# A fused sparse-attention and gated-FFN kernel: first gate weights in two column pieces, 52 constant matmuls in a new order, the last product in halves

## The chip, the cores and the metric

The kernel runs on one core of a Trainium2 chip. The metric is the device time of one execution in microseconds. Before the change three runs gave a median of 281.0 us (280.67 to 282.69). One more execution was recorded by the hardware profiler; it took 279.88 us, with a span of 278.2 us from the first to the last instruction.

TensorE (PE) multiplies matrices, VectorE (DVE) and ScalarE (ACT) do elementwise work and move results out of the accumulator banks, GpSimd (POOL) does elementwise work more slowly, and SyncE (SP) issues most transfers. Transfers run in queues: SP's loads and stores in one (q1 in the profile), the weight loads that POOL issues in another (q0).

## The reference

Two steps follow each other. The first is causal attention over 4 batches, 8 heads, 768 positions and a head size of 64, in which every query sees only six chunks of 32 keys:

- per chunk the minimum and the maximum of each key component are taken; a bound for query and chunk is `sum(max(q * k_min, q * k_max))`
- per query the six chunks with the highest bounds among those not ahead of it are kept
- softmax of `q k^T / 8` over the kept chunks and the causal positions, times `v`

The heads are put side by side, so that there are 3072 rows `x` of 512. The second step is a gated feed-forward layer, `(sigmoid(x @ w_gate) * (x @ w_val)) @ w_out`, with 1536 features.

## The kernel before

**Units.** The 3072 rows are cut into eight units of 384. Unit 0 holds the first 128 rows of batches 0, 1 and 2; for these every chunk is among the kept six, so they need no selection (`first`, line 699). The other units take three blocks of 128 rows each. A unit goes through: turning keys and queries so that the head dimension lies on the partitions (transposes `kT`, `qT`, for unit 0 `kfT`, `qfT`), bounds and choice of chunks (`ub`, `ubn`, `mx`, `ap`, `apt`), scores (`sc`), exponentials on ACT (`exp`), the causal mask on POOL (`cm`), the product with the values (`pv`), division (`rz`, `x`), a turn of the result (`xps` and `xT`; for units 3 to 7 a DMA transpose issued by SP), and the feed-forward layer (`ffn`, line 1239).

**Feed-forward layer.** The 1536 features are 12 blocks of 128. For each there is a gate product `g` and a value product `v` of four matmuls (384 columns), a tanh on ACT in place of the sigmoid, and a product on DVE (`hg`, line 1280). Then `o` multiplies by `w_out`. Units 5 to 7 compute the gate blocks 2 to 9 in pairs with seven block products instead of eight (`by7`). Units 4 to 7 compute the output by a seven-product scheme as well (`pair`, line 1058): once for two row blocks of the unit, and for the third blocks of two units together (`u45`, `u67`). A scheme's products are p1, p2 and p6, p5, p3, p7, p4; each is evacuated by an addition on DVE onto an array of four quarters (`c11`, `u4`, `c12`, `c22`, `c21`), and the last of all is p4 of `u67`, then `c21`, then the last store.

**Loads.** SP loads raw k, q and v. POOL issues the weight loads, which turn float32 into float16 on the way: `wgp` and `wg0` (the first four gate blocks), `wv0`, `wv1`, `wg1`, `wv2`, `wg2`, then `wo0` to `wo2`. `wg`, `wv` and `wo` with a number are 512 columns (or 4 blocks of 128 rows) each.

**Constant matmuls.** `keep_awake` (line 589) adds 30 matmuls of a constant with itself, named `fl`. Their results aren't read; they only keep PE at work while the first data come.

**What sets the order.** Each operation is named and added to a plan with its reads and writes. Three written tables then decide: `ORDER` (line 96) gives the order in which all operations are issued and the engine of each, `SLOTS` the buffer slot of each buffer, and `TIES` adds waits of one operation for another. Every engine works through its own part of `ORDER` in that order; dependencies are kept by semaphores. So a name's place in `ORDER` is its place in its engine's queue, and a waiting operation holds all behind it on its engine.

In the order before, PE starts with nine constant matmuls; then the transposes of the first keys and queries, the first scores and the other constant matmuls follow. The first gate products are `g_u0_0` and `g_u0_2`, then the bounds of unit 1 (`ub_u1`), `g_u0_3`, `g_u0_1`, and the value products from `v_u0_1` on. On POOL `wgp` stands between two causal masks of the first unit, and `wg0` and `wv0` three operations later, behind `hkf0`.

Of the kernel before, what the change touches and what calls it, by code (L numbers as in the profile page):

```python
# [96 lines left out]
ident=G ones16=V fl_4=P fl_2=P fl_8=P fl_3=P fl_1=P fl_0=P fl_29=P k2_u1=S kn_u1_2=A qf1_0=S kf1_0=S kf0_0=S fl_6=P fl_5=P epat0=V  # L97
ident16=V ap0=V epat=G hkp110=A hkp000=A hkp001=V kT_u1_2=P kcr0=V kt_u1_2=V hk0_u1_2=G vf1_1=G hkp011=V hkp010=G vf1_2=G hkp100=G
kf1_2=S kf0_1=S kfT_0=P kxf1=V fl_17=P fl_10=P fl_7=P kx0_u1_2=V kf16_0=V qf0_0=S qfT_0=P qf16_0=V qf1_1=S kf1_1=S kfT_1=P
kf16_1=V fl_15=P fl_16=P scf_0=P expf_0_1=A fl_19=P qf0_1=S qfT_1=P hq0=V ap1=V fl_14=P fl_9=P fl_13=P fl_11=P fl_18=P fl_12=P  # L100
qf16_1=V scf_1=P v10=G vf_0=S v16_0_0=G qf0_2=S qf1_2=S kf0_2=S expf_0_0=A cmf_0_0=G pvf_0_0=P rzf_0_0=V xf_0_0=V kx1_u1_2=V
cmf_0_1=G wgp=G kfT_2=P pvf_0_1=P qfT_2=P qf16_2=V rzf_0_1=V xf_0_1=V kxf0=V expf_1_0=A cmf_1_0=G vf_1=S vc_1=G pvf_1_0=P
rzf_1_0=V xpsf_0_0=P expf_1_1=A cmf_1_1=G pvf_1_1=P hkf0=G hk1_u1_2=A kf16_2=A scf_2=P expf_2_1=A expf_2_0=A k0_u1=S kn_u1_0=V
kT_u1_0=P xf_1_0=V fl_20=P fl_21=P wg0=G q3_u1=S qn_u1_3=A q2_u1=S rzf_1_1=V xf_1_1=V xpsf_1_1=P hq1=V xTf_1_1=V kx0_u1_0=V
kx1_u1_0=V vf_2=S wv0=G cmf_2_0=G fl_23=P xpsf_0_1=P fl_24=P fl_22=P fl_27=P xpsf_1_0=P vc_2=G xTf_1_0=V pvf_2_0=P rzf_2_0=V
xf_2_0=V q1_u1=S k3_u1=S kn_u1_3=G kT_u1_3=P hkp111=A q0_u1=S fl_28=P kx1_u1_3=V cmf_2_1=G pvf_2_1=P xpsf_2_0=P rzf_2_1=V xf_2_1=V
qT_u1_3=P qf_u1_3=V k1_u1=S qn_u1_1=A qT_u1_1=P xTf_0_0=A xTf_0_1=A qn_u1_2=A qn_u1_0=A kn_u1_1=G kT_u1_1=P kx1_u1_1=V kx0_u1_1=V
kt_u1_0=A qm_u1_3=A fl_25=P xpsf_2_1=P fl_26=P qT_u1_2=P v_0_3=S v_0_2=S v_0_1=S qf1_3=S k0_u2=S q2_u2=S k1_u2=S qf_u1_1=V
qf_u1_2=V v11=G wv1=G wg1=G hq0_u1_3=G qT_u1_0=P kt_u1_3=A hk0_u1_3=G hq1_u1_3=G wv2=G xTf_2_1=A xTf_2_0=A qf_u1_0=A qm_u1_0=A
g_u0_0=P g_u0_2=P kx0_u1_3=V kcr_f=V kcr_u1=V hkp101=V hq1_u1_0=V hkf1=V kt_u1_1=V hk0_u1_1=G wg2=G qm_u1_2=A qm_u1_1=A ub_u1=P  # L110
ubn0_u1=V ubm0_u1=V hq0_u1_1=A hq0_u1_2=A g_u0_3=P g_u0_1=P mx0_u1=V ap0_u1=V apt0_u1=V hqm0_u1_0=V v_u0_1=P v_u0_0=P v_u0_2=P
hq0_u1_0=A tanh_u0_2=A tanh_u0_1=A hg_u0_1=V ubn1_u1=V v_u0_3=P tanh_u0_3=A hg_u0_3=V ubm1_u1=V hg_u0_2=V tanh_u0_0=A hg_u0_0=V
hk0_u1_0=A hq1_u1_1=A sc_u1_0_2=P exp_u1_0_2=A sc_u1_1_2=P sc_u1_0_1=P sc_u1_0_0=P exp_u1_1_2=A sc_u1_1_0=P sc_u1_1_1=P
exp_u1_0_0=A exp_u1_0_1=A v_u0_7=P wo0=G hqm0_u1_2=G sc_u1_2_2=P exp_u1_2_2=A sc_u1_2_0=P exp_u1_2_0=A sc_u1_3_0=P sc_u1_3_2=P
exp_u1_3_2=A exp_u1_1_0=A sc_u1_3_1=P exp_u1_3_1=A exp_u1_3_0=A v16_0_3=G wo1=G v_u0_4=P sc_u1_2_1=P v_u0_6=P exp_u1_2_1=A
hk1_u1_0=G v16_0_2=G wo2=G mx1_u1=V ap1_u1=V apt1_u1=V hqm1_u1_0=V g_u0_5=P tanh_u0_5=A v_u0_5=P exp_u1_1_1=A hqm1_u1_2=A g_u0_6=P
tanh_u0_6=A g_u0_7=P tanh_u0_7=A hg_u0_7=V v16_0_1=G cm_u1_3=G pv_u1_3=P cm_u1_2=G hk1_u1_1=G g_u0_4=P tanh_u0_4=A hg_u0_4=V
vf1_3=G hq1_u1_2=G pv_u1_2=P sc_u1_5_1=P sc_u1_4_2=P sc_u1_4_1=P rz_u1_1=V x_u1_1=V exp_u1_4_1=A v_u0_9=P v_u0_10=P xps_u1_1=P
xT_u1_1=A exp_u1_4_2=A hg_u0_6=V hk1_u1_3=V hg_u0_5=V v_u0_8=P g_u0_10=P tanh_u0_10=A kcr1=V hg_u0_10=V g_u0_8=P tanh_u0_8=A
hg_u0_8=V sc_u1_5_2=P exp_u1_5_2=A g_u0_9=P tanh_u0_9=A hg_u0_9=V sc_u1_4_0=P exp_u1_4_0=A cm_u1_1=G pv_u1_1=P cm_u1_0=G qn_u2_2=G  # L120
sc_u1_5_0=P pv_u1_0=P exp_u1_5_0=A sc_u1_6_1=P exp_u1_6_1=A sc_u1_6_2=P exp_u1_6_2=A exp_u1_5_1=A sc_u1_7_2=P sc_u1_7_0=P
g_u0_11=P qT_u2_2=P sc_u1_7_1=P tanh_u0_11=A exp_u1_7_2=A exp_u1_7_0=A exp_u1_7_1=A kn_u2_1=V kT_u2_1=P rz_u1_0=V x_u1_0=V
xps_u1_0=P cm_u1_5=G pv_u1_5=P cm_u1_4=G pv_u1_4=P qf_u2_2=V q1_u2=S qn_u2_1=V qT_u2_1=P sc_u1_6_0=P kt_u2_1=A exp_u1_6_0=A
kn_u2_0=G kT_u2_0=P kt_u2_0=A v_u0_11=P rz_u1_2=V xT_u1_0=V x_u1_2=V xps_u1_2=P q3_u2=S qn_u2_3=G qT_u2_3=P cm_u1_7=G pv_u1_7=P
# [1332 lines left out]
```

## Time and profile before

| | us |
|---|---|
| median of three runs | 281.0 |
| profiled execution | 279.88 |
| its span | 278.2 |
| PE busy | 269.2 |
| DVE busy | 231.2 |
| ACT busy | 180.4 |
| POOL busy | 163.1 |

A row of the profile names the line in the kernel, the engine, the operation, what it writes and reads (output<-input, buffer numbers left out), and how often it occurs. In a timeline the first number is the start in us, the second the length; square brackets give idle time of the engine ahead of it and what ended it. A waiting row reads "who <- for whom: us in total, times, longest". In the chain that ended last each piece has a start, a length and an engine or transfer. A row of transfers reads: output<-input, issuing engine, count, KB, and the time from issue to landing.

### The profile page before, as it was taken

To read this page: it belongs to the slowest core of one execution; us is meant where nothing else is said; L and a number is where in the kernel's file an instruction comes from. 1 tells how busy PE (TensorE), PEld (TensorE's weight loads), DVE (VectorE), ACT (ScalarE), POOL (GpSimd) and SP (SyncE) were. 2 spreads that over 40 slices of the span, in tenths; PEclk is the share of its full clock that TensorE was granted. 3 is DMA by queue.
4 is the path that set the end of the run, shared out by engine and by line. 5 is a ranking of instruction groups with operands and counts; after the bars stand their busy time and mean duration, and the time that the engine had idled before them with its cause. 6 is when DMAs were issued, how large, how long until landed. Compare 5 with 4: busy or idle time off the path is not lost.

```text
span 278.2 us, 7566 instructions
## 1 busy us (share of the span) xinstructions
PE 269.2 (97%) x2806; PEld 189.3 (68%) x2806; DVE 231.2 (83%) x686; ACT 180.4 (65%) x386; POOL 163.1 (59%) x262
## 2 busy tenths in 40 slices
PE   5979999999999999999999999999999999999995
PEld 3755658667755666557687657776888688778684
DVE  4799747687999998796999987978889998888985
ACT  6388969569858944468689979988983422341430
POOL 5797744639372873534669966724766467163440
PEclk9999999999999999999999999999999999999999
DMA  6999999999999598696896230100320033000304
GB/s 157 258 281 204 207 217 208 220 179 202 187 217 189 142 183 188 145 161 125 164 157 114 68 85 17 40 0 3 73 77 2 1 83 127 2 1 2 151 2 152
DMA packets 131717, 34.70 MB, mean 125 GB/s; under 512 B 119776, under 2 KB 128736, under 8 KB 131680
## 3 DMA queue, kind: packets, MB, share of 16 engines
q1 hardware_dynamic: 126912, 29.50, 50.6%
q0 software_dynamic: 4768, 4.72, 10.1%
q8 instruction: 22, 0.36, 0.5%
q14 instruction: 15, 0.12, 0.1%
HBM read 30.67 MB, written 6.29 MB: 133 GB/s over the span
## 4 chain that ended last, share of the span: by engine, by line
PE 87%; DMA 6%; DVE 5%; SPq 1%; issue 0%; POOL 0%; DVEq 0%
PE v_u L1259 20%; PE g_u L1259 15%; PE sc_u L957 12%; PE o_u L1308 11%; PE p_u L1082 10%; PE pv_u L990 7%; DMA wg<-in_moe_w_gate_dram 5%; PE p_g_u L1191 5%; PE ube_u L896 3%; DMA kf<-in_k_dram 1%; DVE xf L768 1%; PE kfT L709 1%; PE qfT L709 1%; PE fl L591 1%; DVE kx_u L681 1%; DVE kcr L681 1%
## 5 line engine op out<-in xcount | busy, mean ns | idle before, releaser
L968 ACT ACTIVATE att_u<-sc_u 128x512 f16<-128x512 f32 (+3 forms) x184 | 86.9, 573 | 8.6 <-PE sc_u L957 7.3
L1259 PE MATMUL v_u<-xT_u,wv 128*128 128x384 f16 x384 | 72.4, 326 | 0.0
L1280 DVE SCALAR_TENSOR_TENSOR hg_u<-gate_u,v_u 128x384 f16<-128x384 f16 x96 | 51.2, 545 | 19.3 <-ACT gate_u L1271 9.7
L1271 ACT ACTIVATE gate_u<-g_u 128x384 f16<-128x384 f32 x72 | 35.1, 499 | 40.3 <-PE g_u L1259 35.1
L1259 PE MATMUL g_u<-xT_u,wg 128*128 128x384 f16 x288 | 56.0, 326 | 0.9 <-ACT xT_u L452 0.5
L1259 PEld LDWEIGHTS <-wv 128*128 128x128 f16 x384 | 36.2, 98 | 20.3 <-issue 0.2
L974 POOL TENSOR_SCALAR_AFFINE_SELECT att_u<-att_u 128x384 f16<-128x384 f16 (+1 forms) x56 | 28.0, 509 | 37.4 <-ACT att_u L968 16.4
L1259 PEld LDWEIGHTS <-wg 128*128 128x128 f16 x288 | 26.7, 98 | 18.3 <-DMA wg<-in_moe_w_gate_dram 1.8
L1308 PE MATMUL o_u<-wo,hg_u 128*128 128x512 f16 x144 | 34.3, 379 | 0.0
L990 PE MATMUL pv_u<-v,att_u 128*128 128x65 f16 x640 | 26.3, 193 | 0.0
L990 PEld LDWEIGHTS <-att_u 128*128 128x128 f16 x640 | 24.2, 98 | 2.9 <-issue 0.6
L1228 DVE TENSOR_TENSOR f_g_u<-p_g_u,f_g_u 128x192 f32<-128x192 f32 (+1 forms) x72 | 24.9, 383 | 1.0 <-PE p_g_u L1191 0.4
L957 PE MATMUL sc_u<-hqe,hke 128*128 128x128 f16 (+2 forms) x220 | 25.1, 243 | 0.0
L957 PE MATMUL sc_u<-hqo,hko 128*128 128x128 f16 (+2 forms) x220 | 24.1, 243 | 0.0
L1308 PEld LDWEIGHTS <-hg_u 128*128 128x128 f16 x144 | 13.7, 98 | 13.4
L957 PEld LDWEIGHTS <-hke 128*128 128x128 f16 x220 | 16.5, 98 | 4.9 <-issue 0.6
L957 PEld LDWEIGHTS <-hko 128*128 128x128 f16 x220 | 16.4, 98 | 4.4
L673 POOL CAST v<-v 128x512 f16<-128x512 f32 x23 | 14.4, 627 | 5.8 <-DVE qf_u L863 1.8
L1271 ACT ACTIVATE gate_u<-f_g_u 128x384 f16<-128x384 f32 x24 | 11.9, 519 | 5.6 <-DVE hg_u L1280 2.9
L1011 DVE TENSOR_TENSOR x_u<-pv_u,rz_u 128x384 f16<-128x384 f32 (+1 forms) x28 | 14.6, 524 | 0.9 <-DMA xT_u<-x_u 0.6
L919 DVE MAX8 mx_u<-ubn_u 128x8 f32<-128x8 f32 (+16 forms) x152 | 12.7, 158 | 0.3
L1099 DVE SCALAR_TENSOR_TENSOR sw<-p_u,sw 128x256 f32<-128x256 f32 (+1 forms) x20 | 10.6, 528 | 2.4 <-PE p_u L1082 2.0
(187 smaller groups left out, 504.9 us busy)
## 6 DMA issues: line engine op xcount, KB each, us to landing
v<-in_v_dram SPq DMA_DIRECT2D x23, 256.0 KB, 4.7
k<-in_k_dram SPq DMA_DIRECT2D x12, 384.0 KB, 5.4
q<-in_q_dram SPq DMA_DIRECT2D x12, 384.0 KB, 5.9
out_dram<-osb_u SPq DMA_DIRECT2D x12, 256.0 KB, 3.3
out_dram<-sw SPq DMA_DIRECT2D x8, 256.0 KB, 2.1
wv<-in_moe_w_val_dram POOLq DMA_DIRECT2D x3, 512.0 KB, 9.8
wo<-in_moe_w_out_dram POOLq DMA_DIRECT2D x3, 512.0 KB, 17.6
qf<-in_q_dram SPq DMA_DIRECT2D x8, 128.0 KB, 3.3
```

The lines of the kernel that those rows point to most:

```text
L673: plan.add(f"v16_{b}_{ib}", {POOL: pool(H * D)}, lambda e: nc.gpsimd.tensor_copy(v16[b % 2][:, ib, :, 0:D], at(t)), reads=[t], writes=[("v ...
L957: nc.tensor.matmul(at(t)[:, o:o + 128 * m], hk[b % 2][e_][:, p, 128 * jb:128 * jb + 128], hq[u.side][e_][:, p, 128 * x:128 * (x + m)], sta ...
L968: plan.add(f"exp_{u.name}_{h}_{y}", {ACT: act(n)}, lambda e, t=t, att=att, b0=b0, n=n: nc.scalar.activation(at(att)[:, b0:b0 + n], at(t), ...
L974: nc.gpsimd.affine_select(out=dv, in_=dv, compare_op=ALU.is_ge, fill=0.0, base=0, pattern=[[0, u.m], [1, 128]], channel_multiplier=-1)
L990: nc.tensor.matmul(at(pv)[:, last, x, :], at(att)[:, c:c + 128], v16[b % 2][:, jb, h, :], start=(jb == 0), stop=(jb == ib))
L1011: plan.add(f"x_{u.name}_{p}", {DVE: dve(u.t)}, lambda e: nc.vector.tensor_tensor(at(x_).rearrange("p a (e d) -> p e a d", e=2), at(pv)[:, ...
L1082: nc.tensor.matmul(at(to)[:, side], a(j)[:, i], b(j)[:, i], start=j == i == 0, stop=j == 2 and i == 1)
L1228: plan.add(f"{p}_{name}", {POOL: pool2(192 * n), DVE: dve(192 * n)} if slow else {DVE: dve(192 * n)}, lambda e: both(e).tensor_tensor(dst( ...
L1259: nc.tensor.matmul(at(t), w16[:, c, 128 * fb:128 * fb + 128], at(u.xt)[:, c, :], start=(c == 0), stop=(c == 3))
L1271: plan.add(f"tanh_{u.name}_{fb}", {ACT: act(T, not seven[0])}, lambda e, gv=gv, gate=gate: nc.scalar.activation(at(gate), gv(), AF.Tanh, s ...
L1280: plan.add(f"hg_{u.name}_{fb}", {DVE: dve(T)}, lambda e, vv=vv, gate=gate, hg=hg, fb=fb: nc.vector.scalar_tensor_tensor(at(hg)[:, fb % 2], ...
L1308: nc.tensor.matmul(at(o), at(hgs[fc // 2])[:, fc % 2, 128 * tb:128 * tb + 128], wo16[:, fc, lo:hi], start=(fc == 0), stop=(fc == NFB - 1))
```

## The change

There are five edits.

1. The first gate block's load was cut along the 512 rows of the contraction: `wgp` took the first 128 rows, `wg0` the other 384. Now it is cut along the features: `wgp` takes columns 0 to 255 of all rows, `wg0` columns 256 to 511. A gate product of feature blocks 0 and 1 reads the first piece, one of blocks 2 and 3 the second.
2. There are 52 constant matmuls instead of 30.
3. In `pair`, for `u67` alone, the last product p4 is computed in two halves of 128 columns with a bank each (`p4`, `p4b`), each with its own addition (`c21`, `c21b`) and its own store (`out_u67_1`, `out_u67_1b`). The store of the side piece (`out_u67_b1`) stands ahead of them, as before. Each half is issued as one operation of six matmuls.
4. `ORDER`, `SLOTS` and `TIES` are written anew. 66 operations change their engine; the number of operations goes from 701 to 723 on PE, from 540 to 529 on DVE, from 385 to 391 on ACT, from 256 to 262 on POOL and from 128 to 129 on SP; the ties from 137 to 129. On PE 26 constant matmuls come first, then the transposes of unit 1's and unit 0's first keys and queries. All 52 stand ahead of the first gate product. The first gate products are now `g_u0_1`, `g_u0_0` and `g_u0_3`, then `ub_u1`, `g_u0_2` and the value products from `v_u0_1` on. On SP unit 0's queries come before unit 1's and unit 0's keys, and the raw values of unit 0 (`vf_0` to `vf_2`) come later among the keys and queries. On POOL `wgp`, `wg0` and `wv0` stand directly behind each other, behind `hkf0`; `wo1` and `wo2` stand behind the causal masks of unit 1's first four heads.
5. The sums of gate weights for the seven-product scheme and that scheme itself would wait for both pieces if they used the first blocks; they don't.

The diff, without the tables:

```diff
-    for i in range(30):
+    for i in range(52):
         keep_awake(i)
...
     def weights(i, prio, after):
         lo, hi = 512 * i, 512 * i + 512
-        c0 = 0
+        mid, part = lo, 4
         if i == 0:
-            c0 = 1
-            plan.add("wgp", {POOL: (760, 760)}, lambda e: nc.gpsimd.dma_start(wg16[:, 0:1, lo:hi], wgs[:, 0:1, lo:hi]),
-                     writes=[("wg", 0, "first")], prio=prio, dma=(750, 2048))
-        return plan.add(f"wg{i}", {POOL: (760, 760)}, lambda e: nc.gpsimd.dma_start(wg16[:, c0:, lo:hi], wgs[:, c0:, lo:hi]),
-                 reads=after, writes=[("wg", i)], prio=prio, dma=(750 * (4 - c0), 2048)), plan.add(f"wv{i}", ...
+            mid, part = lo + 256, 2
+            plan.add("wgp", {POOL: (760, 760)}, lambda e: nc.gpsimd.dma_start(wg16[:, :, lo:mid], wgs[:, :, lo:mid]),
+                     writes=[("wg", 0, "first")], prio=prio, dma=(1500, 2048))
+        return plan.add(f"wg{i}", {POOL: (760, 760)}, lambda e: nc.gpsimd.dma_start(wg16[:, :, mid:hi], wgs[:, :, mid:hi]),
+                 reads=after, writes=[("wg", i)], prio=prio, dma=(750 * part, 2048)), plan.add(f"wv{i}", ...
...
-        product("p4", p4, 0, lambda j: block(j, 1, 1), t_(3), lambda j: h(1, 1)(j) + [(tw, 3, j)])
-        onto("c21", p4, 1, slice(2, 3), lambda: four()[:, 2:3], [key[2]])
         if name == "u67":
             store(f"{name}_b1", lambda: four()[:, 3], rows[1], 256, 512, [key[3]], next_)
-            store(f"{name}_1", lambda: four()[:, 2], rows[1], 0, 256, [key[2]], next_)
+            for side, cut, last in (("", slice(0, 128), p4), ("b", slice(128, 256), bank("p4b"))):
+                def emit(e, cut=cut, last=last):
+                    for j in range(3):
+                        for i in range(2):
+                            nc.tensor.matmul(at(last)[:, 0, cut], block(j, 1, 1)[:, i], t_(3)(j)[:, i, cut], start=j == i == 0, stop=j == 2 and i == 1)
+
+                plan.add(f"p4{side}_{name}", pe(6 * (128 / 2.4 + 4.5)), emit, reads=..., writes=[last], prio=next_())
+                done = key[2] if side == "" else (okey, 2, side)
+                plan.add(f"c21{side}_{name}", {DVE: dve(128)}, lambda e, cut=cut, last=last: nc.vector.scalar_tensor_tensor(
+                    four()[:, 2, cut], at(last)[:, 0, cut], 0.5, four()[:, 2, cut], ALU.mult, ALU.add),
+                    reads=[last, key[2]], writes=[done], prio=next_(EV))
+                store(f"{name}_1{side}", lambda cut=cut: four()[:, 2, cut], rows[1], cut.start, cut.stop, [done], next_)
         else:
+            product("p4", p4, 0, lambda j: block(j, 1, 1), t_(3), lambda j: h(1, 1)(j) + [(tw, 3, j)])
+            onto("c21", p4, 1, slice(2, 3), lambda: four()[:, 2:3], [key[2]])
             store(f"{name}_1", lambda: four()[:, 2:4], rows[1], 0, 512, [key[2], key[3]], next_)
...
                 op = plan.add(f"g_{u.name}_{fb}", pe(650), product(g, wg16), 
-                    reads=xt + [("wg", fb // 4)] + [("wg", 0, "first")] * (fb < 4), writes=[g],
+                    reads=xt + [("wg", 0, "first") if fb < 2 else ("wg", fb // 4)], writes=[g],
```

555 lines of the change are left out of this document (280 added, 275 removed).

## The prediction

> **What bounds the kernel now.** I read the page's busy times and the stretches first, because they say where TensorE is not busy; only there can time be won.
>
> ```profile
> PE 269.2 (97%) x2806; PEld 189.3 (68%) x2806; DVE 231.2 (83%) x686; ACT 180.4 (65%) x386; POOL 163.1 (59%) x262
> ...
> 0.00:6.50 6.50, 3.67 (x16) 2.42 (x17) 3.17 (x8) 4.34 (x4) 3.50 (x11) 1.00 0.66 153
> 6.50:10.00 3.50, 3.50 (x19) 2.30 (x19) 2.87 (x5) 0.29 (x1) 3.27 (x5) 1.00 1.06 238
> 10.00:16.00 6.00, 5.05 (x61) 3.84 (x57) 4.26 (x12) 3.26 (x6) 4.79 (x9) 1.00 1.08 281
> 16.00:22.80 6.80, 5.22 (x52) 4.03 (x49) 6.45 (x21) 6.53 (x15) 6.65 (x12) 1.00 1.22 252
> 22.80:40.40 17.60, 17.25 (x156) 10.25 (x155) 12.66 (x49) 13.75 (x33) 10.11 (x19) 1.00 1.21 209
> ...
> 51.00:274.30 223.30, 223.30 (x2385) 158.36 (x2384) 194.12 (x577) 143.38 (x306) 128.99 (x199) 1.00 0.50 103
> 274.30:278.20 3.90, 0.61 (x6) 0.30 (x4) 1.11 (x2) 0.00 (x0) 0.00 (x0) 0.98 0.40 141
> ```
>
> The first two numbers of a stretch row are its bounds, then its length and PE's busy time; the last two are the DMA share and GB/s. From 51.00 to 274.30 us PE is busy for all of 223.30 us. A new order of that stretch can lose time there, but wins none unless it removes work. PE's gaps lie in the front (2.83 + 0 + 0.95 + 1.58 = 5.4 us before 22.80), in 0.35 us up to 40.40, and in the last 3.3 us. From 6.5 us on the front's DMA share is above 1, so there transfers are a second limit. Next come the waits, the chain and the engines' timelines.
>
> ```profile
> PE g_u L1259 <- DMA wg<-in_moe_w_gate_dram: 0.2, 1, 0.2
> ...
> 26.18 14.22 DMA wg<-in_moe_w_gate_dram
> 40.45 1.48 PE g_u L1259 x8
> ...
> 42.90 0.28 PE pv_u L990 x9
> ...
> 22.82 1.76 PE L1259 MATMUL g_u<-xT_u,wg 128*128 128x384 f16 x8 [0.51 <-ACT xT_u L452]
> ...
> 25.75 1.47 PE L1259 MATMUL g_u<-xT_u,wg 128*128 128x384 f16 x8
> 27.06 2.76 PE L1259 MATMUL v_u<-xT_u,wv 128*128 128x384 f16 x16
> ...
> 12.82 0.79 POOL L610 DMA_DIRECT2D wg<-in_moe_w_gate_dram  x1
> ...
> 15.91 0.80 POOL L612 DMA_DIRECT2D wg<-in_moe_w_gate_dram  x1
> 16.70 0.78 POOL L613 DMA_DIRECT2D wv<-in_moe_w_val_dram  x1
> ...
> wg<-in_moe_w_gate_dram POOLq DMA_DIRECT2D x1, 128.0 KB, 5.5
> wg<-in_moe_w_gate_dram POOLq DMA_DIRECT2D x1, 384.0 KB, 7.3
> wv<-in_moe_w_val_dram POOLq DMA_DIRECT2D x1, 512.0 KB, 9.8
> ```
>
> The last three rows give each issue's time to landing. Added to the issue, the first gate piece lands at 12.82 + 5.5 = 18.3, the rest of the first gate block at 15.91 + 7.3 = 23.2, the first value block (wv0) at 16.70 + 9.8 = 26.5, and the last gate block (wg2) at 26.18 + 14.22 = 40.40. PE uses them at 22.82, at once behind that, at 27.06 and at 40.45. So from 22.8 to 40.5 us PE runs on the heels of the weights, and the chain, which goes through wg2, says the same. What the first gate product gains by starting early comes back as a wait unless the weights come early too.
>
> **The change part by part.**
>
> *Two gate pieces.* Before, every product of the first four blocks needed both pieces. In the new order the first two products (blocks 1 and 0) need the first piece alone, then block 3 the second. Ahead of the first value product stand, as before, four gate products and the bounds. From the rows, 25.75 to 27.06 is two products, 0.65 us each. The bounds lie between the first pair and the second: 25.75 - 22.82 = 2.93 less 1.3 leaves 1.6, with some 0.4 of waiting in it, so 1.2. The first value product is then ready 4 x 0.65 + 1.2 = 3.8 us after the first gate product: at 26.6 if that stays at 22.82, at 24.9 if it comes at 21.1. But wv0 lands at 26.5. So it starts near 26.6 in both cases, 0.45 us earlier than 27.06.
>
> Does wv0 still land at 26.5? In the new order of POOL's queue the first piece stands where the second one stood (15.91 in the old trace), 3 us later than 12.82, and the second piece and wv0 stand directly behind it; wv0 is one issue (0.8 us) later, less what the chain ahead of it gains. The queues' own rows say what that is worth (packets, MB, share of 16 engines; 12 to 20 us first, then 20 to 24 us):
>
> ```profile
> q1 hardware_dynamic: 4999, 2.13, 97.7%
> q0 software_dynamic: 222, 0.21, 16.7%
> ...
> q0 software_dynamic: 729, 0.73, 110.2%
> ```
>
> Until 20 us SP's queue (q1) fills the engines and POOL's (q0) moves only 0.21 MB; then q0 moves 0.18 MB per us. A later start cedes at most 0.21 MB to q1, which then is done so much sooner. I take no shift of wv0; bounds: 1.2 us later (0.21 / 0.18, nothing given back) and, if SP's loads drain sooner, 1.2 us earlier. The two pieces have rows of 256 columns, half as long, so 1024 packets for 512. One of q0's takes 1.102 x 64 / 729 = 97 ns of an engine; q1's, of 426 bytes, 0.977 x 128 / 4999 = 25 ns, so smaller packets aren't dearer per byte. I take 0; if a half packet took as long as a whole one it would be 512 x 97 / 16 ns = 3.1 us.
>
> Then wg2. Between the first value product and the first gate product on wg2 the old trace has 40.45 - 27.06 = 13.4 us, less the wait of 0.25. The new order places the same fifteen feature products there, and one group of attention-times-value matmuls (0.28 by its row) and one 256-column score product (some 0.1) more: 0.38 us. 26.6 + 13.15 + 0.38 = 40.1: PE again waits for wg2 at 40.4, but with 0.38 us more work behind it. **Front: -0.4 us.** The last weight block, issued at 31.99, landed 19.1 us later, at 51.1, and its product ran at 51.82; 0.4 earlier still leaves 0.3.
>
> ```profile
> 31.99 0.75 POOL L618 DMA_DIRECT2D wo<-in_moe_w_out_dram  x1
> ...
> wo<-in_moe_w_out_dram POOLq DMA_DIRECT2D x1, 512.0 KB, 19.1
> ...
> 51.82 1.03 PE L1308 MATMUL o_u<-wo,hg_u 128*128 128x512 f16 x4
> ```
>
> POOL now issues the last two output blocks behind four causal masks, the last of them tied to the first unit's block 5. That block's gate product stands 3.5 us of PE work ahead of the first product on wg2, and its gate and product take 1.05 us more (rows below): near 38 us. The block ahead of them (26.91 + 17.1, 44.0) still occupies the queue then, so this costs nothing; the cover is 6 us.
>
> *22 more constant matmuls.* All 52 stand ahead of the first gate product, 26 of them at PE's head instead of 9.
>
> ```profile
> 0.00:6.50 6.50, 2.10 (x9) 1.22 (x10) 1.00 0.66 153
> ...
> 5.81 1.09 PE L709 MATMUL kfT<-ident,kf 128*128 128x128 f32 x4 [0.90 <-DMA kf<-in_k_dram]
> ...
> 12.89 0.63 PE L709 MATMUL kfT<-ident,kf 128*128 128x128 f32 x4
> ```
>
> Nine took 2.10 us, 0.23 each, so 22 more are at most 5.1 us, inside the front's 5.4 us of idle time. Behind them queue the first transposes: the 26 end by 1.12 + 26 x 0.23 = 7.1 us, 1.3 us past the first transposed block of keys of the old trace. Cost 0 while wv0 binds (first gate product up to 22.8); without that cover 1.3 us. Against that, the same four transposes took 1.09 us at 5.81 and 0.63 at 12.89, though the clock column reads 1.00 in both: PE ran slower at the start.
>
> The Trainium skill (TensorE: Matmul & The Clock Gate, Part 1: The HAM clock gate) says that PE runs at half rate until about 3.4 us of sustained work. By that the 26 would bring full rate before the first transposes, whose 1.09 would become 0.63. The two durations agree with it; the granted clock in the rows doesn't show it.
>
> *The rest of the new order.* By the two lists DVE loses 11 operations, POOL and ACT gain 6 each, SP's and POOL's queues are reshuffled (the DMA transposes in other places among the loads), and buffers get other slots. PE's work is the same. DVE has 194.12 of 223.30 us there (87%), so a late DVE result is what would make PE wait. I take 0, since nothing in the lists lengthens a chain; below 0 it can't go, PE having no gap. Above: a wait costs at most a gate and its product on ACT and DVE,
>
> ```profile
> L1280 DVE SCALAR_TENSOR_TENSOR hg_u<-gate_u,v_u 128x384 f16<-128x384 f16 x96 | 51.2, 545 | 19.3 <-ACT gate_u L1271 9.7
> L1271 ACT ACTIVATE gate_u<-g_u 128x384 f16<-128x384 f32 x72 | 35.1, 499 | 40.3 <-PE g_u L1259 35.1
> ```
>
> 0.50 + 0.55 = 1.05 us; three of them 3.1 us.
>
> *Last product in halves.*
>
> ```profile
> 274.10 0.82 PE L1082 MATMUL p_u<-tw,hg_u 128*128 128x256 f16 x6
> ...
> 274.30 0.70 DVE ox L1099
> ...
> 275.09 0.42 DVE ox L1099
> ...
> 275.01 0.86 SPq L1127 DMA_DIRECT2D out_dram<-ox  x2
> ...
> L1127 SPq DMA_DIRECT2D out_dram<-ox x5: 332/333/448, 257.1 to 275.5; - x5
> L1099 DVE SCALAR_TENSOR_TENSOR ox<-p_u,ox x5: 425/425/692, 272.3 to 275.1; 128x256 f32<-128x256 f32 x3, 128x512 f32<-128x512 f32 x2
> ...
> out_dram<-ox SPq DMA_DIRECT2D x1, 256.0 KB, 2.0
> out_dram<-ox SPq DMA_DIRECT2D x2, 128.0 KB, 1.7
> ```
>
> The product ends at 274.92, but its addition starts at 275.09, behind the wide addition on DVE (274.30 to 275.00). Halving the product wins nothing: the same columns in 12 matmuls, all hidden under the wide addition. DVE: 256 columns 0.425, 512 columns 0.692, so 128 columns some 0.29; the halves end at 275.38 and 275.67 instead of 275.51. SP issues now three stores: the side piece at 275.01 (0.33), the first half at 275.34, the second at 275.67 to 275.79, where the last one now starts at 275.87 - 0.45 = 275.42. So the last issue is 0.25 to 0.37 later. Landing goes from 2.0 to 1.7 with half the bytes, so 64 KB perhaps 1.55. **Tail: +0.2 us** (0 to 0.4).
>
> The Trainium skill (DMA: Bandwidth & Descriptors, Anatomy of one DMA) has a transfer at about 2.0 us fixed plus bytes over 436 GB/s, fitted on POOL's queue; an estimate from it for 64 KB is 2.15 us, and the tail would then be 0.7 to 0.8 later. The trace's 1.7 us for 128 KB is below that, so its own step decides.
>
> *Sum.* -0.4 + 0.2 + 0 = -0.2 on the profiled execution's 279.88 us (span 278.2 plus 1.68 around it): 279.7. The median of the three runs, 281.0, lies 1.1 above that execution, so I forecast 280.8, in effect no change. Their spread, 280.67 to 282.69, makes 1% (2.8 us) about what a measurement can tell.
>
> **The rivals.**
>
> *Weights late, slower.* One mechanism: the first two pieces, later by 3 us and in half packets, hold up the one queue in which all later blocks stand. It decides once wv0 lands past 27.0. At the full price of 3.1 us wg2 lands at 43.5 and PE waits: 3.1 less 0.4 of moved work, plus 0.2 of the tail, is 2.9; 279.88 + 2.9 + 1.1 = 283.9 on the median's scale. For: from 24 us on each block comes 3.5 us behind the last, with no slack. Against: bytes, not starts, filled the engines.
>
> *Front early with the weights, faster.* If SP's loads drain sooner and the early clock helps, the first gate product comes at 21 and the blocks 1.2 us earlier: -0.4 - 1.2 + 0.2, so 279.88 - 1.4 + 1.1 = 279.6. At most 26.6 - 24.9 = 1.7 us beyond the 0.4. Against: the engines were full from 6.5 us on.
>
> *New waits in the middle.* Two of 1.05 us: 280.8 + 2.1 = 282.9; three, 283.9. For: 66 operations change engine and DVE is 87% busy. Against: it loses work.
>
> *The halves do what their name says:* the tail shorter, not longer. It would take an issue that costs SP nothing; then 0 in place of 0.2, which nobody can measure.
>
> **How the numbers follow.** No change (with the tail either way) 0.55, 280.0 to 281.9 by its own bounds and the runs' scatter; front early 0.14; weights late 0.13, half of it past 283.8; new waits 0.18, a third past 283.8. The range, 279.4 to 283.7, takes in all but the ends of the rivals. Slower by over 1%: 0.065 + 0.06, so 0.13; faster by over 1% (below 278.2) needs more than the front has, 0.03; within 1% 0.84.
>
> **What would show it.** Right: the first value product near 26.6, a wait for wg2 near 40.4, no PE gap from 51 us, three stores at the end with the last issued near 275.7 less the front's gain. Wrong: wv0 landing past 27.0 or before 25.5; a value or gate product that waits for its buffer in the long stretch; transposes before 9 us that still take 1.09 and push the first gate product past 22.8.

## The result: slower by about 1%

The changed kernel takes 283.75 us (median of four runs, 283.64 to 285.44), the kernel before 280.84 beside it (280.21 to 282.69). The ratio is 1.0106, with a 95% interval of 1.0078 to 1.0134: slower. The forecast was 280.8 and its range ended at 283.7; the result lies 0.05 above the range and 2.9 above the forecast.

The profiled execution of the changed kernel took 285.44 us with a span of 283.7. It is the longest of its four (the other spans are 281.9, 282.1 and 281.9), while the profiled execution of the kernel before, with 278.2, was a short one. So the two traces lie 5.5 us apart where the medians lie 2.9 apart, and what differs between executions of one kernel has to be told from what is always there.

The granted clock helps with that. Over the profiled execution it was 0.992 of full speed, over the other three 0.999, 0.998 and 0.999. One stretch of 3.80 us at 0.55 (its row stands in the last section) is 1.7 us of clock, 0.006 of the span; the other three lack at most 0.002, some 0.6 us. So that slow stretch belongs to the profiled execution and not to the median. Whether it is what makes this span 1.6 to 1.8 us longer isn't shown.

From the page of the changed kernel, TensorE's busy time; then the stretches of the prediction, cut at the places that answer to them (bounds, length, busy time of PE, PEld, DVE, ACT and POOL, granted clock, DMA share, GB/s):

```profile
PE 272.4 (96%) x2834; PEld 191.1 (67%) x2834; DVE 229.1 (81%) x675; ACT 184.5 (65%) x392; POOL 164.4 (58%) x268
...
16.00:22.80 6.80, 3.88 (x39) 2.98 (x37) 6.59 (x18) 6.56 (x17) 6.71 (x12) 1.00 1.13 226
22.80:40.40 17.60, 16.24 (x121) 8.84 (x122) 10.51 (x40) 11.58 (x28) 9.98 (x19) 0.90 1.22 207
51.00:279.40 228.40, 228.30 (x2432) 161.06 (x2430) 197.34 (x581) 148.29 (x317) 130.02 (x206) 1.00 0.50 103
```

From 51 us on TensorE still shows no gap worth naming (0.1 us). The idle time has grown from 16 to 40.4 us, and in 22.80 to 40.40 the granted clock is 0.90 where it was 1.00. The waits of TensorE and its timeline say why; POOL's issues and their landings (last number of a transfer row: us from issue) follow:

```profile
PE g_u L1274 <- DMA wg<-in_moe_w_gate_dram: 2.0, 1, 2.0
PE pv_u L993 <- POOL v L676: 1.1, 1, 1.1
...
23.25 3.79 PE L1274 MATMUL g_u<-xT_u,wg 128*128 128x384 f16 x12 [1.98 <-DMA wg<-in_moe_w_gate_dram]
...
15.60 1.00 POOL L613 DMA_DIRECT2D wg<-in_moe_w_gate_dram  x1
16.59 0.76 POOL L615 DMA_DIRECT2D wg<-in_moe_w_gate_dram  x1
17.34 0.76 POOL L616 DMA_DIRECT2D wv<-in_moe_w_val_dram  x1
25.41 0.74 POOL L615 DMA_DIRECT2D wg<-in_moe_w_gate_dram  x1
...
wg<-in_moe_w_gate_dram POOLq DMA_DIRECT2D x1, 256.0 KB, 7.6
wg<-in_moe_w_gate_dram POOLq DMA_DIRECT2D x1, 256.0 KB, 8.8
wv<-in_moe_w_val_dram POOLq DMA_DIRECT2D x1, 512.0 KB, 11.6
wg<-in_moe_w_gate_dram POOLq DMA_DIRECT2D x1, 512.0 KB, 17.7
```

`wgp` lands at 15.60 + 7.6 = 23.2, the second piece at 25.4, `wv0` at 28.9 (26.5 before) and `wg2` at 43.1 (40.4 before). TensorE is done with its transposes at 21.3, stands idle for 1.98 us, and its first 12 gate matmuls then take 3.79 us, where 8 took 1.47 in the kernel before.

**Where the 5.5 us are.** The same marks in both kernels, the first value product, the bounds of unit 2, the bounds of unit 3 and TensorE's end, cut the rest of the span into three stretches. First the kernel before, then the changed one:

```profile
27.06:55.37 28.31, 28.06 (x262) 18.88 (x259) 18.75 (x62) 21.45 (x53) 15.88 (x31) 1.00 1.16 213
55.37:81.72 26.35, 26.35 (x302) 18.10 (x301) 23.47 (x63) 20.20 (x47) 15.02 (x28) 1.00 1.08 196
81.72:274.92 193.20, 193.19 (x2061) 137.84 (x2060) 167.95 (x505) 121.17 (x256) 111.41 (x166) 1.00 0.41 87
```

```profile
29.03:58.95 29.92, 28.64 (x262) 18.96 (x261) 19.45 (x66) 20.86 (x51) 16.18 (x31) 1.00 1.10 203
58.95:84.69 25.74, 25.74 (x298) 17.60 (x297) 23.04 (x61) 21.67 (x48) 16.23 (x32) 1.00 1.07 194
84.69:279.39 194.70, 194.61 (x2071) 138.46 (x2070) 168.32 (x502) 122.62 (x260) 108.74 (x166) 1.00 0.41 87
```

| where | worked out from | us |
|---|---|---|
| first value product later | 29.03 - 27.06 | +1.97 |
| waits up to the bounds of unit 2 | (29.92 - 28.64) - (28.31 - 28.06) | +1.03 |
| TensorE busier there | 28.64 - 28.06 | +0.58 |
| up to the bounds of unit 3 | 25.74 - 26.35 | -0.61 |
| from there to TensorE's end | 194.70 - 193.20 | +1.50 |
| TensorE's end to the span's end | (283.7 - 279.39) - (278.2 - 274.92) | +1.03 |
| sum | | +5.50 |

The minus in the fourth row is a value product (`v_u1_7`, 0.65 us) that the new `ORDER` puts behind the bounds of unit 3; it comes back in the fifth. Over the three stretches together TensorE's busy time is 28.64 + 25.74 + 194.61 = 248.99 us against 28.06 + 26.35 + 193.19 = 247.60: 1.4 us more, with the same matmuls in another order.

This extra busy time is made of waits too short to show as idle. The row of a product of four matmuls of 384 columns lasts 0.81 us, while the next product can start 0.65 us behind its start; so a wait of up to some 0.16 us leaves no gap. Start times show it. A value product and the product of `by7` behind it, first in the kernel before, then in the changed kernel, with the additions of VectorE that it waits for:

```profile
236.06 0.81 PE L1259 MATMUL v_u<-xT_u,wv 128*128 128x384 f16 x4
236.72 0.33 PE L1191 MATMUL p_g_u<-xT_u,wg 128*128 128x192 f16 x2
```

```profile
239.82 1.21 DVE L1102 SCALAR_TENSOR_TENSOR ox<-p_u,ox 128x256 f32<-128x256 f32 x2
240.28 0.81 PE L1274 MATMUL v_u<-xT_u,wv 128*128 128x384 f16 x4
241.08 0.33 PE L1206 MATMUL p_g_u<-xT_u,wg 128*128 128x192 f16 x2
```

In the one kernel the second product starts 0.66 us behind the first, in the other 0.80, just behind the additions' end at 239.82 + 1.21 = 241.03. Behind the bounds of unit 3 the changed kernel's trace has five such places, 0.10 to 0.25 us each and 0.77 in all (start to start, above the median for the same kind of matmul); four of them wait for VectorE's additions, one for a mask of POOL. The kernel before has none there. Ahead of those bounds such short waits add up to 1.1 us, and to 0.5 before.

**The end.** The changed kernel's last additions and its stores:

```profile
278.76 0.69 DVE L1102 SCALAR_TENSOR_TENSOR ox<-p_u,ox 128x512 f32<-128x512 f32 x1 [0.16 <-PE p_u L1085]
279.55 0.29 DVE L1132 SCALAR_TENSOR_TENSOR ox<-p_u,ox 128x128 f32<-128x128 f32 x1
279.76 0.28 DVE L1132 SCALAR_TENSOR_TENSOR ox<-p4b_u,ox 128x128 f32<-128x128 f32 x1
...
279.48 1.33 SPq L1142 DMA_DIRECT2D out_dram<-ox  x3
...
out_dram<-ox SPq DMA_DIRECT2D x2, 64.0 KB, 1.6
```

The additions take what was worked out (0.29 and 0.28). The last of the three issues starts at 280.40, 1.64 us behind the start of the wide addition (278.76); before it was 275.42 - 274.30 = 1.12. From its start to the end of the span it takes 3.3 us, before 278.2 - 275.42 = 2.8. So 0.5 of the 1.03 us is the third issue, and 0.5 comes behind it.

### The profile page after: what moved, and what is told of

It is laid out like the page before. It is cut to its first block, busy times and chain, and to the rows that moved or that the text cites. A ratio compares the mean times of both kernels' runs of the same rounds, so it can differ in the third digit from the quotient of the medians.

```text
span 283.7 us, 7633 instructions
## 1 busy us (share of the span) xinstructions
PE 272.4 (96%) x2834; PEld 191.1 (67%) x2834; DVE 229.1 (81%) x675; ACT 184.5 (65%) x392; POOL 164.4 (58%) x268
## 4 chain that ended last, share of the span: by engine, by line
PE 81%; DMA 6%; DVE 3%; POOL 3%; ACT 2%; SPq 2%; issue 1%; DVEq 0%; ACTq 0%
PE v_u L1274 18%; PE g_u L1274 15%; PE o_u L1323 11%; PE sc_u L960 10%; PE p_u L1085 9%; PE pv_u L993 6%; PE p_g_u L1206 5%; DMA wg<-in_moe_w_gate_dram 3%; PE ube_u L899 2%; PE fl L594 2%; DMA q<-in_q_dram 2%; DMA vf<-in_v_dram 1%; ACT att_u L971 1%; SPq L660 1%; POOL hqo L459 1%
## 5 line engine op out<-in xcount | busy, mean ns | idle before, releaser
L1274 PE MATMUL g_u<-xT_u,wg 128*128 128x384 f16 x288 | 57.9, 333 | 2.0 <-DMA wg<-in_moe_w_gate_dram 2.0
L1274 PEld LDWEIGHTS <-wg 128*128 128x128 f16 x288 | 27.4, 100 | 20.3 <-issue 3.3
L993 PE MATMUL pv_u<-v,att_u 128*128 128x65 f16 x640 | 27.0, 193 | 1.1 <-POOL v L676 1.1
L993 PEld LDWEIGHTS <-att_u 128*128 128x128 f16 x640 | 24.8, 98 | 3.7 <-issue 1.2
L960 PE MATMUL sc_u<-hqe,hke 128*128 128x128 f16 (+2 forms) x220 | 25.4, 243 | 0.2
L960 PE MATMUL sc_u<-hqo,hko 128*128 128x128 f16 (+2 forms) x220 | 25.1, 243 | 0.0
```

The costliest lines, as they stand in the source:

```text
L960: nc.tensor.matmul(at(t)[:, o:o + 128 * m], hk[b % 2][e_][:, p, 128 * jb:128 * jb + 128], hq[u.side][e_][:, p, 128 * x:128 * (x + m)], sta ...
L993: nc.tensor.matmul(at(pv)[:, last, x, :], at(att)[:, c:c + 128], v16[b % 2][:, jb, h, :], start=(jb == 0), stop=(jb == ib))
L1274: nc.tensor.matmul(at(t), w16[:, c, 128 * fb:128 * fb + 128], at(u.xt)[:, c, :], start=(c == 0), stop=(c == 3))
```

## The experiments

The theories. **A:** the weights come late (the rival "weights late"), through column pieces, through a late start, or through what SyncE's loads do in the new order. **B:** the new order has a loss of its own, waits or a busier TensorE. **C:** the halves at the end. Each kernel ran beside the kernel before; a ratio is to that.

### Undoing the parts

**e1_rows**: the changed kernel with the first block cut along the rows again.

```diff
-            mid, part = lo + 256, 2          # wgp, wg0: 256 columns each
+            c0 = 1                           # wgp: 128 rows, wg0: 384 rows
...
-   reads=xt + [("wg", 0, "first") if fb < 2 else ("wg", fb // 4)]
+   reads=xt + [("wg", fb // 4)] + [("wg", 0, "first")] * (fb < 4)
```

> The changed kernel with the first gate block cut along the rows again (128 rows, then 384), all else as changed. Late start (the pieces are issued 3 us later than before, so the whole weight queue is late): the first value block still lands near 28.9 us, time 283.3 to 283.9. Half packets (1024 short packets in place of 512 cost about 0.9 us): the first value block lands near 28.0, time near 282.8. New order alone: 283.7, and the first value product still near 29.

Measured: 285.7 us, ratio 1.0141 (1.0073 to 1.0208), above what each theory had. `wv0` landed at 27.2 and `wg2` at 41.3, 1.7 us earlier than in the changed kernel, and yet nothing was won: the wait of the products of attention and values for POOL's cast of unit 0's values, 1.1 us in the changed kernel, was now 2.8. TensorE came there earlier, and the cast, which now waited for SP's load of these values, started at 40.55 instead of 40.10.

```profile
PE pv_u L993 <- POOL v L676: 2.8, 1, 2.8
PE g_u L1274 <- DMA wg<-in_moe_w_gate_dram: 1.6, 1, 1.6
```

That the earlier weights are what held this load back isn't shown.

**e4_cols**: the kernel before, its own order, with the column pieces alone (the edit of e1_rows the other way).

> The kernel before with the first gate block cut along the columns, in its own order (the first two gate products, blocks 0 and 2, then still need both pieces). Late start: the issues stay at 12.8, 15.9 and 16.7 us, so no change, 280.5 to 281.2. Half packets: the first value block lands 0.9 later, near 27.4, and PE waits: 281.6.

Measured: 282.04 us, ratio 1.0034 (0.9989 to 1.0079). `wv0` landed at 17.13 + 11.4 = 28.5, 2.0 us later, and `wg2` at 42.3, 1.9 later. The issue of `wv0` was 0.4 later, its way from issue to landing 1.6 longer. So the column pieces delay the weights by themselves; of that 0.7 us reached the median (281.82 without the longest of the ten runs, 285.8, against 281.16), and the interval includes none.

**e3_whole**: the changed kernel with the last product whole. **e5_halves**: the kernel before with the halves.

```diff
-for side, cut, last in (("", slice(0, 128), p4), ("b", slice(128, 256), bank("p4b"))): ...
+product("p4", p4, 0, ...); onto("c21", p4, 1, slice(2, 3), ...); store(f"{name}_1", ..., 0, 256, ...)
```

> The changed kernel with the last product whole again, one addition and one store fewer. If the third store at the end costs what the changed trace shows from the wide addition's end to the span's end (4.25 us in place of 3.2): 1.0 us less, 282.7. If it costs what the prediction said: 0.2 less, 283.5. If the halves help: more than 283.8.

> The kernel before with the last product in two halves, two additions and one more store, all else as before. By the changed trace's end (wide addition to the span's end 4.94 us in place of 3.90): 1.0 us more than before, about 282.0. By the prediction's working: 0.2 more, 281.2. By the run that made the changed kernel's product whole (0.5 less): 281.6.

Measured: e3_whole 283.24 us, ratio 1.0063 (1.0030 to 1.0096), 0.5 below the changed kernel; e5_halves 281.84, ratio 1.0014 (0.9997 to 1.0031), 0.5 above the kernel before. From the start of the wide addition to the end of the span the traces have 3.92 without halves and 5.02 with them (3.90 and 4.94 in the two kernels). Both ways round the halves cost 0.5 us on the medians and 1.0 to 1.1 in the traces. The medians alone don't prove it: the interval of e5_halves just includes none, and that of e3_whole overlaps the changed kernel's. The traces, two with halves and two without, show the 1.0 both times.

**e6_order**: the changed kernel with row pieces and a whole last product, so that the new `ORDER`, `SLOTS` and `TIES` with 52 constant matmuls are left alone.

> The changed kernel with the row pieces and the whole last product of before: the new order with its 52 constant matmuls alone. If the pieces and the tail are all there is: 281.2, as before. If the order itself lacks cover (the values cast of unit 0 late, the wait in front of the second attention product): 1.0 below the run with row pieces alone, near 284.5, with a wait of 1 to 2.8 us of that product on GpSimd's cast.

Measured: 284.9 us, ratio 1.0131 (1.0062 to 1.0199). The new order by itself loses as much as the whole change. It keeps the late issue of the weights and SP's new order, which are part of `ORDER`. `wv0` landed at 27.5; the first gate product waited 2.2 us, the next 11 matmuls took 3.50, and the wait of 1.1 for the cast was there.

```profile
24.19 3.50 PE L1249 MATMUL g_u<-xT_u,wg 128*128 128x384 f16 x11 [2.21 <-DMA wg<-in_moe_w_gate_dram]
...
59.59:85.33 25.74, 25.74 (x298) 17.61 (x297) 23.05 (x61) 21.68 (x48) 16.19 (x32) 1.00 1.05 191
85.33:279.90 194.57, 194.56 (x2065) 138.36 (x2064) 167.24 (x502) 122.54 (x260) 109.14 (x166) 1.00 0.41 88
```

The last two rows are those of the changed kernel to 0.15 us. From the bounds of unit 3 to TensorE's end, eight other kernels with the new order but for the front had 194.56 to 194.60 (the two with 12 more constant matmuls, below, 194.96 and 195.19), and every kernel with the old order 193.19 to 193.21. This part, 0.7 us without the moved value product, doesn't depend on how the weights arrive.

With row pieces the new order lies 4.5 us (e1_rows) and 3.6 (e6_order) above the kernel before that ran beside it, with column pieces 2.9 (the changed kernel) and 2.1 (e3_whole). So in the new order the column pieces cost no time, though they delay `wv0` in the old one; the intervals overlap, and whether they help isn't shown.

**e8_fl30**: the changed kernel with 30 constant matmuls.

```diff
-    for i in range(52):
+    for i in range(30):
```

> The changed kernel with 30 constant matmuls (the 22 new ones left out wherever they stand, 17 instead of 26 at PE's head). If they are hidden: no change, 283.4 to 284.0. If they hold up the first transposes: up to 1 us less, 282.8. If they keep PE's rate up: up to 1.5 us more, 285.

Measured: 284.15 us, ratio 1.0095 (1.0067 to 1.0123), as the changed kernel. The 22 are hidden.

### When the weights start

**e2_early**: the changed kernel with the first three weight loads issued earlier on POOL.

```diff
-cmf_0_0=G ... cmf_0_1=G ... cmf_1_0=G ... hkf0=G wgp=G wg0=G wv0=G
+cmf_0_0=G wgp=G ... cmf_0_1=G wg0=G ... cmf_1_0=G wv0=G ... hkf0=G
```

> The changed kernel with its three first weight loads issued earlier on GpSimd, one each behind the first three causal masks (near 11, 13.5 and 14.5 us in place of 15.6, 16.6 and 17.3). Late start: the first value block lands near 26.5, all later blocks 2 to 2.5 us earlier than in the changed kernel, time 281.2 to 281.8. Half packets: the short packets remain, so the gain is at most 1.5 us, 282.2 or more. New order alone: no gain, 283.5.

Measured: 288.38 us, ratio 1.0264 (1.0164 to 1.0364), far above what each theory had. `wv0` landed at 24.9, 4 us earlier, and the first gate product came at 26.67, 3.4 us later than in the changed kernel: the transposes it needs waited for copies of queries and keys, and these for SP's loads of unit 1 (1.74 us of idle time on ScalarE, 4.48 on GpSimd).

```profile
PE qT_u L785 <- ACT qn_u L442: 1.7, 1, 1.7
PE pvf L750 <- POOL vh L446: 1.6, 1, 1.6
PE kT_u L785 <- POOL kn_u L446: 1.3, 1, 1.3
```

**e9_wgplate**: the kernel before with `wgp` alone issued later.

```diff
-cmf_0_1=G wgp=G ... cmf_1_1=G hkf0=G
+cmf_0_1=G ... cmf_1_1=G hkf0=G wgp=G
```

> Kernel before with one issue moved: the first gate piece (row piece, 128 KB) behind hkf0, about 2.3 us later, near 15.1, so that 0.13 MB of the weight queue's work before 16 us is given up. Theory A (the late start of the weights alone makes the new order slow): wv0 lands 0.7 to 1.2 us later than 26.5, wg2 near 41.3 to 41.6, TensorE waits for its first gate product, time +0.7 to +1.5 against the kernel before. Rival B (a later start is given back by the other queue, as the prediction had it; the new order of SyncE's loads and of the engines' work around them is what delays): wv0 within 0.3 of 26.5 and the time within 0.4 of before.

Measured: 280.92 us, ratio 1.0018 (0.9987 to 1.0049). `wgp` was issued at 14.73 instead of 12.82; `wv0` landed at 16.29 + 10.7 = 27.0 instead of 26.5, `wg2` at 41.3. The traces lie 0.8 us apart, the medians 0.1 the other way. A late first piece alone, in the old order, cost 0.8 in the traces and nothing in the medians (the interval reaches to 1.4 us): `wv0`'s 0.5 lies between the numbers of the two theories, the time is rival B's.

**e11_wgpfirst**: the changed kernel with `wgp` where the kernel before had it (behind `cmf_0_1`).

> Changed kernel with the first gate piece (256 columns) issued where the kernel before issued its own first piece, behind the second causal mask, near 12.9 instead of 15.6; the second piece and wv0 stay where they are and come one issue earlier in the queue. Theory A (late start): wgp lands near 20, wv0 1 to 2 us earlier than 28.9, time 1 to 1.5 below the changed kernel. Rival B (the engines were full anyway, so SyncE's loads of unit 1 give back what the weights win, as when all three pieces were issued 4 us earlier): first gate product earlier by under 1 us or later, time within 0.7 of the changed kernel or above.

Measured: 285.23 us, ratio 1.0149 (1.0110 to 1.0188). `wgp` landed at 20.1, `wv0` at 26.8 and `wg2` at 40.9: the weights were back at the old times, and the kernel wasn't faster. TensorE waited for no weights, but its transposes waited 1.1 us for ACT's copy of queries, which waited for SP's load of them; the first value product came at 27.83.

```profile
PE qT_u L785 <- ACT qn_u L442: 1.1, 1, 1.1
...
19.48 0.93 ACT L442 COPY qn_u<-kq_u 128x384 f32<-128x384 f32 x2 [1.57 <-DMA kq_u<-in_q_dram]
...
27.83:58.19 30.36, 28.63 (x262) 18.95 (x260) 19.81 (x68) 20.85 (x51) 18.16 (x35) 1.00 1.08 202
83.93:278.53 194.60, 194.59 (x2071) 138.48 (x2070) 167.24 (x502) 122.54 (x260) 109.17 (x166) 1.00 0.41 87
```

So late weights are no sufficient account of the loss. With them in time there remain, in this trace, 0.77 of start, 30.36 - 28.31 = 2.05 up to the bounds of unit 2, 194.60 - 193.20 - 0.61 = 0.8 behind, and the end.

### The waits that the new order has

**e7_untied**: the changed kernel without the tie `v16_0_1<hg_u0_4`, which held POOL's third cast of values behind a product of DVE.

> The changed kernel without the tie that lets GpSimd's cast of unit 0's first values wait for DVE's product of block 4. If this tie is a wait of its own: the 1.06 us gap in front of the second attention product goes, time 282.7. If the late weights (last gate block at 43.1) are the next limit anyway: the gap goes, and a wait for the last gate block takes its place, 283.3 to 283.7.

Measured: 284.92 us, ratio 1.0113 (1.0061 to 1.0166). The wait of TensorE was 1.3 instead of 1.1: without the tie the cast waits for the load itself.

```profile
40.41 0.61 POOL L659 CAST v<-v 128x512 f16<-128x512 f32 x1 [1.68 <-DMA v<-in_v_dram]
```

**e12_pvlater**: the changed kernel with the waiting products behind two value products.

```diff
-pv_u1_2=P pv_u1_3=P rz_u1_1=V sc_u1_4_2=P ... v_u0_10=P v_u0_9=P
+sc_u1_4_2=P ... v_u0_10=P v_u0_9=P pv_u1_2=P pv_u1_3=P rz_u1_1=V
```

> Changed kernel with TensorE's products of attention and values that waited 1.06 us for GpSimd's cast of unit 0's values (pv_u1_2, pv_u1_3, with rz_u1_1 behind them) moved behind three score products and two value products (about 1.7 us of work). Theory A (the losses add up, and the 1.06 is one of them): the wait of pv_u1 for v is gone, the time 0.8 to 1.1 below the changed kernel, near 282.8. Rival B (the wait is a place where TensorE would have waited for wg2 or its other inputs anyway): another wait of about 1 us takes its place before 52 us, the time within 0.3 of the changed kernel.

Measured: 285.01 us, ratio 1.0149 (1.0114 to 1.0184). The wait is gone, and another has taken its place shortly ahead of it: the gate products on the second block wait 0.87 us for weights that landed at 36.8 here, 36.0 in the changed kernel.

```profile
PE g_u L1261 <- DMA wg<-in_moe_w_gate_dram: 1.7, 3, 0.9
...
36.92 2.77 PE L1261 MATMUL g_u<-xT_u,wg 128*128 128x384 f16 x16 [0.87 <-DMA wg<-in_moe_w_gate_dram]
```

From the first value product to the bounds of unit 2 it took 30.39 us, not less than the 29.92 of the changed kernel. Theory A's gain is refuted; the new wait is the one of rival B, though the time is 1.3 above the changed kernel, which B doesn't explain.

### The clock behind the idle time

**e10_awake**: the changed kernel with 22 of the first 26 constant matmuls moved to directly ahead of `g_u0_1`. **e14_awake12**: the changed kernel with 12 more there, all in one accumulator bank. **e13_three**: e14's and e12's edits with a whole last product.

> Changed kernel with 22 of TensorE's 26 first constant matmuls moved to directly ahead of the first gate product, where TensorE stood idle for 2 us and then ran 12 gate matmuls in 3.79 us. Theory A (the first value block binds: it landed at 28.9 and its product began at 29.03): the gate products take 2.0 to 2.6 us instead of 3.8, but a wait for wv0 of 1.5 to 2 us takes their place, time within 0.5 of the changed kernel. Rival B (the half clock is a loss of its own): the time 1.5 us below the changed kernel, near 282.2. If the 22 are too many (0.13 each, 2.8 us, against 2 us of idle time) the first gate product is up to 0.8 later, which theory A hides too.

> Changed kernel with 12 more constant matmuls (64) directly ahead of the first gate product, all in the bank which that product uses, which is free then; the others stay. 12 x 0.12 us is 1.4 us of the 2 us in which TensorE waits for the first gate piece. Theory A (the first value block, landing at 28.9, binds): the first 12 gate matmuls take 2.0 to 2.4 us instead of 3.79, a wait for wv0 takes the place, the first value product stays within 0.3 us of the landing of wv0 and the time within 0.5 of the changed kernel. Rival B (the half clock costs time of its own): 1.2 to 1.6 below the changed kernel.

> Changed kernel with three edits together: the last product whole, the products of attention and values behind the value products, and 12 more constant matmuls ahead of the first gate product. If the account of the loss is right (0.5 to 1.0 for the halves, 1.06 for the cast, and what is left is the late weights and 1.4 us that the same matmuls take longer in the new order), the time is 281.7 to 282.4, still above the kernel before by 0.5 to 1.3. If it is at the kernel before or below, the 1.4 us are not lost.

Measured: 290.02 us, ratio 1.0305 (1.0262 to 1.0347); 286.86, 1.0233 (1.0198 to 1.0267); 286.72, 1.0211 (1.0163 to 1.0259). Of e10 and of e14:

```profile
26.04 3.54 PE L581 MATMUL fl<-ones 128*128 128x256 f16 x19 [0.80 <-DVE kt_u L444]
29.63 2.11 PE L1261 MATMUL g_u<-xT_u,wg 128*128 128x384 f16 x12
```

```profile
22.42 3.86 PE L582 MATMUL fl<-ones 128*128 128x256 f16 x12
26.34 2.11 PE L1262 MATMUL g_u<-xT_u,wg 128*128 128x384 f16 x12
```

In both kernels the gate matmuls behind the constant ones ran at full rate (12 in 2.11 us instead of 3.79), but the constant ones cost more than that: in e10 they waited 3.1 us for their banks and then took 3.5; in e14 the 12 took 3.86 us, 0.32 each, where 12 in different banks had taken 1.47 elsewhere in the changed kernel. The first value product came at 33.6 and 30.3, behind its weights (28.0 and 29.0), so neither run tells what the half clock costs by itself; both theories missed. e13's number was to be the sum of the parts, and as two of its three edits didn't do what they were made for, it isn't that. This is left open.

## Why the prediction was wrong, step by step

Two steps failed: "I take no shift of wv0", and the 0 for the rest of the new order. For the time the second weighs more, since the new order lost as much without the column pieces and the halves (e6_order).

**Front, -0.4 us: wrong in sign.** The step that failed is "I take no shift of wv0". It landed 2.4 us later, between 27.7 and 29.0 in the seven other traces with column pieces and a front as in the changed kernel or nearly so (e3, e7, e8, e10, e12, e13, e14). That is past the 27.0 from which the rival "weights late" decides, and the late first value product follows at 29.03.

Two terms were taken at 0. The start: "a later start cedes at most 0.21 MB", with 1.2 us as its bound; e9_wgplate measured 0.5 us on `wv0`. The half packets: "smaller packets aren't dearer per byte" and "I take 0", with 3.1 us as the upper end; e4_cols measured 2.0 us on `wv0`, 0.4 of it from a later issue. That was the mis-sized term, and the reading behind it was too narrow: it took 25 ns for a packet of SP's queue as the price of a shorter packet of the weight queue. The packets of the two queues between 20 and 22 us, first of the kernel before, then of the changed kernel; the last pair is e6_order from 24 to 26 us:

```profile
q0 software_dynamic: 384, 0.38, 116.7%
q1 hardware_dynamic: 67, 0.02, 3.7%
```

```profile
q0 software_dynamic: 389, 0.19, 75.7%
q1 hardware_dynamic: 681, 0.17, 48.1%
```

```profile
q0 software_dynamic: 311, 0.31, 91.1%
q1 hardware_dynamic: 312, 0.08, 29.9%
```

In 2 us the weight queue moved 384 packets in one kernel and 389 in the other, but half the bytes; in the first it had the engines almost to itself. By itself a half packet takes 0.757 x 32 / 389 = 62 ns of an engine against 97, so 1024 of them for 512 would cost (1024 x 62 - 512 x 97) / 16 ns = 0.9 us. For the rest the last pair offers an account: there the two queues moved the same number of packets, whatever their size, and so they did from 26 to 42 us in both kernels (2367 and 2348 before, 2372 and 2370 after). A queue whose packets are halved would then get less than its former share of the bytes. But that isn't shown for the stretch in which the half packets ran: from 18 to 22 us of the changed kernel SP's queue moved 1684 packets and the weight queue 578. The Trainium skill (DMA: Bandwidth & Descriptors, Queues, rings and completion order) says that each engine takes turns between the queues that have work, a packet at a time; the pair of 311 and 312 agrees, if its packet is the one that the profile counts. The prediction didn't weigh this rule.

**22 more constant matmuls, 0: right** (e8_fl30). The early transposes did run at full rate, four in 0.60 us instead of 1.09, as the clock-gate rule that the prediction weighed would have it, but nothing was won by it.

**The rest of the new order, 0, "below 0 it can't go", above: three waits: the price was inside the bounds, the 0 was wrong.** The reason given for the 0 was that "nothing in the lists lengthens a chain". The lists don't show when a result is ready, and late DVE results did come, as the prediction said they would have to: behind the bounds of unit 3 four of the five short waits are for DVE. They are 0.10 to 0.16 us each, not 1.05, so they appear as busy time and not as gaps. With those ahead of the bounds of unit 2 they make 1.4 us in the profiled execution: 0.6 there and 0.8 behind unit 3. "PE's work is the same" holds for the matmuls, not for their time. Which moved operation makes the additions late wasn't tried. The waits that do show are in the front, and the wait for the cast is of a kind that was named (a product that waits for an operand), but on POOL and behind a load, not on DVE.

**Tail, +0.2 us (0 to 0.4): right in sign, too small.** 0.5 on the medians, 1.0 in the traces. The third issue starts 0.5 later against the wide addition, where 0.25 to 0.37 was worked out; then the term "landing 1.55" is 1.6 and still the span ends 0.5 later behind the issue, which the sum didn't have. The page of the Trainium skill quoted there gave 0.7 to 0.8, nearer to the result, but not by its own terms: 64 KB on SP's queue landed in 1.6 us, below its fixed 2.0, which was fitted on POOL's.

**The rivals.** "Weights late" gave 283.9 and the median is 283.75, but that agreement is partly chance: its price of 3.1 us measured 2.4 on `wv0`, and the order's short waits and a dearer tail made up the sum. With the weights in time (e11_wgpfirst) the loss was still there. "New waits in the middle" came in part: short waits of 0.7 us in all behind unit 3, where two or three of 1.05 were priced. "Front early" is refuted by e2_early, where earlier weights made the first gate product later. "The halves do what their name says" is refuted by e3_whole and e5_halves.

**What stays open.** How the front's part of the loss divides between weights, SP's loads and the half clock: each kernel that mended one of them found another in its place. In the medians 2.9 us are to be divided. The tail has 0.5 of it, and the short waits behind the bounds of unit 3, which are in every trace of the new order, 0.7. Those ahead of unit 2 vary, from 0.2 (e3_whole, e8_fl30) to 0.6 (the changed kernel). So the front has 1.1 to 1.5, against 3.0 in the profiled execution. The trace of e8_fl30, 281.7 us long like the other executions of the changed kernel and without the slow stretch, has 0.68 at the first value product, which starts as `wv0` lands (27.74), and 0.83 of idle time behind it, (29.35 - 28.27) - (28.31 - 28.06):

```profile
27.74:57.09 29.35, 28.27 (x260) 19.03 (x260) 18.89 (x60) 20.31 (x50) 16.86 (x33) 1.00 1.18 217
```

## What to carry to other kernels

Where two queues fill the DMA engines, count packets as well as bytes: a load cut into shorter rows delayed the loads behind it by 2 us here, and issuing the loads earlier (e2_early) made the first product later, which then waited for what the other queue brings. An order written anew cost TensorE half a per cent in waits that show as busy time, so compare start times and not only busy time; a busy TensorE in the old profile bounds what a new order can win, not what it can lose. A last step split in two paid here for one more issue and its completion, and is worth it only where the end waits for the earlier half.

## What was not expected of the hardware

- The two queues moved equally many packets where both had work for long (2372 and 2370 from 26 to 42 us of the changed kernel), though one's were 1 KB and the other's 0.4 KB on average (2.35 and 0.97 MB).
- An idle time of 1.98 us on TensorE was followed by 12 matmuls in 3.79 us instead of about 2.0, at a granted clock that fell to 0.55:

```profile
21.00:23.20 2.20, 0.27 (x4) 0.10 (x1) 2.20 (x6) 2.11 (x6) 1.74 (x3) 1.00 1.36 202
23.20:27.00 3.80, 3.75 (x16) 1.67 (x17) 1.97 (x4) 1.34 (x4) 2.99 (x6) 0.55 1.24 195
```

- In e8_fl30, with an idle time of 0.66 us, the same 12 took 2.36 us. A slow stretch need not follow that wait: in e3_whole it lay ahead of the gate products, on the transposes, and the 12 took 2.65 us.

```profile
19.30:22.60 3.30, 3.30 (x21) 3.13 (x20) 2.12 (x6) 2.52 (x8) 1.79 (x5) 0.50 1.34 202
```

- Twelve constant matmuls into one bank (e14_awake12) took 0.32 us each, against 0.12 in changing banks. In the trace each lasts 0.27 us and starts 0.06 behind the end of the one before, whose buffer it overwrites, and each carries a wait on a semaphore; so the kernel's own order of writes is the likely reason, but it wasn't tried by itself.
